# PV matmuls of two heads on the two column halves of TensorE, with one logarithm and one product for both

**Chip, cores, metric.** One core of a Trainium2 chip; runs of one round share a chip, and each is compared with the kernel before of its own rounds. The metric is the device time of one execution in microseconds (us), median of several.

**Names in the profile lines.** PE is TensorE's matmuls and PEld its weight loads; DVE is VectorE, ACT ScalarE, POOL GpSimd. L311 is line 311 of the kernel. PSUM is the memory to which the kernel's matmuls write; a bank is here one of the two [128 x 512] halves of o_ps. A timeline line gives start, duration (us), engine, line, operation, output<-input, shapes and count, and in brackets the idle time before it and what ended it. A wait line gives its total, how often it came and the longest. The end of a matmul record is modelled, so costs on TensorE are read from start to start.

## The reference

Sliding-window causal attention (window 64) over 8 batches x 8 heads x 576 positions x 64, then a multiplicative feed-forward network (FFN) on the 4608 x 512 result:

```python
scores = scale * q @ k.T;  mask: 0 <= i - j < 64
attn = exp(scores - max) / sum;   x = (attn @ v), heads side by side
out = ((x @ w1) * (x @ w2)) @ w3 @ w_out
```

## The kernel before

It folds `w3 @ w_out` into one matrix at the start, then runs attention and FFN interleaved. Attention goes in 48 **groups** (`d`), each two pairs of heads by 192 queries: `scores(d)` makes masked exponentials `pt`; `values(d)` makes PV (the exponentials times V) and softmax sums, and divides. The sum comes from 64 columns of ones that lie beside each head's V, in the order V0, ones, V1, ones. So a full 128-column weight gives head 0 with values on partitions 0 to 63 and sums on 64 to 127, and head 1 the other way round. Hence two logarithms and two products, each on 64 partitions. Division is `exp(-ln(sum))`.

```python
ps_t = ... bufs=1;  ps_s = ... bufs=1;  ps_v = ... bufs=1;  ps_f = ... bufs=3   # PSUM
# scores(d): two heads on the two halves of the ROWS of TensorE (64 x 128)
for a in range(2):
    nc.tensor.matmul(s_ps[:, a, jj, c0:c0 + n], kT[half, j, k0:k0 + P], qT[half, j, q0:q0 + n], ...)
... exponential on ACT, two masks on POOL ...
def values(d):
    ...
    o_ps = ps_v.tile([P, 2, 512], FP32, name="o_ps")
    for jj in range(2):
        first = True
        for a in range(2):
            c0 = 0
            for bi, (k0, q0, n, _) in enumerate(seg):
                o0 = a * 192 + q0 - q_base
                nc.tensor.matmul(o_ps[:, jj, o0:o0 + n],                       # L311
                                 v16[:, si * 2 + bi, j0 + jj, a * D:a * D + P],
                                 pt[:, a, jj, c0:c0 + n], start=first, ...)
                first = False
                c0 += n
    ...
    nc.scalar.activation(y[0:D], o_ps[D:P, :, 0:192], AF.Ln)                   # L320
    nc.scalar.activation(y[D:P], o_ps[0:D, :, 192:384], AF.Ln)                 # L321
    nc.scalar.activation(r, y, AF.Exp, scale=-1.0)                             # L323
    nc.vector.tensor_tensor(xs[0:D], o_ps[0:D, :, 0:192], r[0:D], ALU.mult)    # L326
    nc.vector.tensor_tensor(xs[D:P], o_ps[D:P, :, 192:384], r[D:P], ALU.mult)  # L327
# FFN: 8 matmuls of 512 columns each for w1/w2 (L395) and for the output (L408)
```

Groups 0 to 11 run in a startup with its own order of work; from group 12 on, a steady schedule has scores and PV half a cycle apart, with FFN matmuls between.

Of the kernel before, what the change touches and what calls it, by code (L numbers as in the profile page):

```python
# [11 lines left out]
ALU = mybir.AluOpType  # L12
AF = mybir.ActivationFunctionType
PSUM = bass.MemoryType.PSUM

P = 128
# [128 lines left out]
def kernel(  # L145
# [11 lines left out]
    nc = tc.nc  # L157
    B, H, S, D = q.shape
# [32 lines left out]
    xT = const.tile([P, NJ, RING], FP16)  # L191
# [104 lines left out]
    def values(d):  # L296
        b, r = divmod(d, 6)
        si, jp = divmod(r, 2)
        j0 = 2 * jp
        v16 = v16s[b % 2]  # L300
        pt = probs.pop(d)
        seg = SEGS[si]
        q_base = seg[0][1]
        o_ps = ps_v.tile([P, 2, 512], FP32, name="o_ps")
        for jj in range(2):
            first = True
            for a in range(2):
                c0 = 0
                for bi, (k0, q0, n, _) in enumerate(seg):
                    o0 = a * 192 + q0 - q_base  # L310
                    nc.tensor.matmul(o_ps[:, jj, o0:o0 + n],  # L311
                                     v16[:, si * 2 + bi, j0 + jj, a * D:a * D + P],
                                     pt[:, a, jj, c0:c0 + n],
                                     start=first, stop=(bi == 1), skip_group_check=True)
                    first = False
                    c0 += n
        if jp == 0:
            lns[b, si] = sb.tile([P, NJ, 192], FP32, name="ln_s", bufs=4)
        y = lns[b, si][:, j0:j0 + 2]
        nc.scalar.activation(y[0:D], o_ps[D:P, :, 0:192], AF.Ln)  # L320
        nc.scalar.activation(y[D:P], o_ps[0:D, :, 192:384], AF.Ln)  # L321
        r = sb.tile([P, 2, 192], FP32, name="r")
        nc.scalar.activation(r, y, AF.Exp, scale=-1.0)  # L323
        x0 = (b * S + q_base) % RING
        xs = xT[:, j0:j0 + 2, x0:x0 + 192]
        nc.vector.tensor_tensor(xs[0:D], o_ps[0:D, :, 0:192], r[0:D], ALU.mult)  # L326
        nc.vector.tensor_tensor(xs[D:P], o_ps[D:P, :, 192:384], r[D:P], ALU.mult)  # L327

    def keep_sums(n):
        b, si = divmod(n, 3)  # L330
# [25 lines left out]
    def tick(u):  # L356

        b, r = divmod(u, 12)
        d = u // 2
        if u % 2 == 0 and d < ND:  # L360
            scores(d)
        ev = late.get(r, [])
        for e in ev:
            if e[0] == "t":
                event(b, *e)
        if u % 2 == 1 and 12 <= d - 1 < ND:
            values(d - 1)
        for e in ev:
            if e[0] != "t":
                event(b, *e)  # L370
        n, m = divmod(u - LAG - 4, 4)
        if m == 3 and n >= 6:
            keep_sums(n)
# [158 lines left out]
    for d in range(5):  # L532
        if d == 0:
            w3Ts[2] = fold_t(2)
        values(d)
        if d < 4:
            scores(d + 2)
        fold_step(d + 2)
        if d == 0:
            load_v(1, 0, 2)  # L540
            load_qk(1, "k", nc.vector.memset)
            load_qk(1, "q")
        if d == 1:
            load_v(1, 3)
        if d == 2:
            copy_v(0, 4)
            for i in range(2):
                load_w12(i, 1)
        if d == 3:
            load_v(1, 4)  # L550
            cast_qk(1, "k", 0, dve_cp)
    cast_qk(1, "k", 1, act_cp)
    cast_qk(1, "q", 0, pool_cp)
    cast_qk(1, "q", 1, act_cp)
    values(5)
    fold_step(7)
    transposes(1, "k", 0, 1, into=spare(ps_s, "s_ps"))
# [113 lines left out]
```

## Time and profile before

| | before |
|---|---|
| median | 296.2 us (295.75 to 296.27) |
| span of the profiled run | 294.3 us |
| TensorE busy | 274.1 us, 93% |
| DVE / ACT busy | 185.4 / 168.4 us |

The costliest-groups list of the kernel before, the lines of `values` (line, engine, operation, output<-input, shapes, count | busy us, mean ns of one | idle before them and its releaser):

```profile
L326 DVE TENSOR_TENSOR xT<-o_ps,r 64x384 f16<-64x384 f32 x48 | 26.4, 550 | 53.8 <-ACT r L323 53.6
...
L320 ACT ACTIVATE ln_s<-o_ps 64x384 f32<-64x384 f32 x48 | 23.4, 487 | 53.4 <-PE o_ps L311 53.3
...
L311 PE MATMUL o_ps<-pt,v 128*128 128x128 f16 (+1 forms) x384 | 27.9, 215 | 5.9 <-DVE xT L327 4.0
...
L327 DVE TENSOR_TENSOR xT<-o_ps,r 64x384 f16<-64x384 f32 x48 | 26.9, 561 | 0.6
...
L321 ACT ACTIVATE ln_s<-o_ps 64x384 f32<-64x384 f32 x48 | 23.1, 482 | 0.5
```

The large idle times of DVE and ACT before these lines cost nothing: those engines are early. The one that counts is TensorE's 4.0 us before L311, waiting for L327.

### The profile page before, as it was taken

What the parts mean: (1) busy time and instruction counts of PE and PEld (TensorE: products, weight loads), DVE (VectorE), ACT (ScalarE), POOL (GpSimd) and SP (SyncE); (2) the same over time, 40 slices, a digit from 0 to 9 for tenths busy, and PEclk for the clock granted to TensorE, in tenths of its full rate; (3) what the DMA queues carried; (4) which work ended last, traced back from release to release, by engine and by line L of the source; (5) the groups of instructions that cost most, each with busy time, mean ns of one, the idle gap of its engine ahead of it and who ended that gap; (6) DMA issues with size and microseconds to landing.
All of it is one profiled execution on the core that took longest, in us unless ns stands there. A gap on an engine that the chain in (4) does not pass through costs nothing.

```text
span 294.3 us, 5925 instructions
## 1 busy us (share of the span) xinstructions
PE 274.1 (93%) x2254; PEld 152.9 (52%) x2254; DVE 185.4 (63%) x289; ACT 168.4 (57%) x281; POOL 180.8 (61%) x214
## 2 busy tenths in 40 slices
PE   7758889898799999999999999999999999999992
PEld 7544555444455555555555787555555445444440
DVE  0715688465787667687777866677867555554541
ACT  2513774676458647766686565487568866642300
POOL 8835995478749856696869463786595344402200
PEclk9999999999999999999999999999999999999998
DMA  6999999990277939094929470950094021012012
GB/s 231 219 181 201 265 278 212 373 131 36 74 266 264 72 110 321 39 85 143 322 20 100 136 295 2 155 73 1 20 171 40 0 74 72 0 38 109 0 57 95
DMA packets 51665, 38.85 MB, mean 132 GB/s; under 512 B 38784, under 2 KB 41856, under 8 KB 51632
## 3 DMA queue, kind: packets, MB, share of 16 engines
q0 software_dynamic: 41744, 9.96, 36.2%
q1 hardware_dynamic: 9888, 28.46, 26.6%
q8 instruction: 19, 0.31, 0.4%
q14 instruction: 14, 0.11, 0.1%
HBM read 38.80 MB, written 9.44 MB: 164 GB/s over the span
## 4 chain that ended last, share of the span: by engine, by line
PE 76%; DVE 6%; ACT 5%; DMA 4%; issue 3%; POOL 3%; POOLq 0%; DVEq 0%; ACTq 0%
PE f_ps L395 38%; PE f_ps L408 19%; PE o_ps L311 7%; PE tp L253 5%; DMA ab<-in_moe_w_dram 4%; PE s_ps L278 4%; DVE xT L327 2%; PE f_ps L454 2%; ACT ln_s L321 2%; ACT r L323 2%; POOL v L488 2%; DVE kT L257 1%; DVE xT L326 1%; ACT ln_s L320 1%; ACT pt L282 1%
## 5 line engine op out<-in xcount | busy, mean ns | idle before, releaser
L395 PE MATMUL f_ps<-xT,w_sb 128*128 128x512 f16 (+1 forms) x640 | 134.1, 358 | 0.0
L290 POOL TENSOR_SCALAR_AFFINE_SELECT pt<-pt 128x512 f16<-128x512 f16 (+1 forms) x64 | 52.1, 814 | 69.0 <-ACT pt L282 68.9
L395 PEld LDWEIGHTS <-w_sb 128*128 128x128 f16 x640 | 59.7, 98 | 50.7 <-issue 0.5
L408 PE MATMUL f_ps<-wc_sb,ab 128*128 128x512 f16 x288 | 67.1, 379 | 0.1
L401 DVE TENSOR_TENSOR ab<-f_ps,a_sb 128x512 f16<-128x512 f32 x72 | 49.8, 692 | 18.4 <-PE f_ps L395 15.8
L326 DVE TENSOR_TENSOR xT<-o_ps,r 64x384 f16<-64x384 f32 x48 | 26.4, 550 | 53.8 <-ACT r L323 53.6
L282 ACT ACTIVATE pt<-s_ps 128x1024 f16<-128x1024 f32 (+1 forms) x48 | 45.5, 949 | 18.0 <-PE s_ps L278 16.5
L400 ACT COPY a_sb<-f_ps 128x512 f32<-128x512 f32 x72 | 41.7, 579 | 24.8 <-PE f_ps L395 23.9
L292 POOL TENSOR_SCALAR_AFFINE_SELECT pt<-pt 128x512 f16<-128x512 f16 (+1 forms) x64 | 52.4, 819 | 4.4
L320 ACT ACTIVATE ln_s<-o_ps 64x384 f32<-64x384 f32 x48 | 23.4, 487 | 53.4 <-PE o_ps L311 53.3
L408 PEld LDWEIGHTS <-ab 128*128 128x128 f16 x288 | 26.9, 98 | 28.8 <-DVE ab L401 0.6
L233 POOL DMA_DIRECT2D v<-in_v_dram x40 | 33.9, 854 | 5.9 <-DMA ab<-in_moe_w_out_dram 4.1
L311 PE MATMUL o_ps<-pt,v 128*128 128x128 f16 (+1 forms) x384 | 27.9, 215 | 5.9 <-DVE xT L327 4.0
L311 PEld LDWEIGHTS <-v 128*128 128x128 f16 x384 | 23.5, 98 | 18.2 <-issue 3.5
L410 DVE COPY t2k<-f_ps 128x512 f32<-128x512 f32 x36 | 24.7, 690 | 11.6 <-PE f_ps L408 11.1
L327 DVE TENSOR_TENSOR xT<-o_ps,r 64x384 f16<-64x384 f32 x48 | 26.9, 561 | 0.6
L323 ACT ACTIVATE r<-ln_s 128x384 f32<-128x384 f32 x48 | 25.1, 523 | 1.5
L321 ACT ACTIVATE ln_s<-o_ps 64x384 f32<-64x384 f32 x48 | 23.1, 482 | 0.5
L278 PEld LDWEIGHTS <-kT 64*128 64x128 f16 x384 | 10.5, 94 | 16.5 <-issue 14.8
L278 PE MATMUL s_ps<-qT,kT 64*128 64x128 f16 (+1 forms) x384 | 18.2, 214 | 0.3 <-ACT pt L282 0.2
L257 DVE COPY kT<-tp 128x768 f16<-128x768 f16 x17 | 16.2, 952 | 0.1
L454 PE MATMUL f_ps<-ab,t2k 128*128 128x512 f16 x64 | 15.0, 379 | 0.4 <-DVE t2k L448 0.3
(59 smaller groups left out, 179.8 us busy)
## 6 DMA issues: line engine op xcount, KB each, us to landing
stage<-in_k_dram SPq DMA_DIRECT2D x16, 576.0 KB
stage<-in_q_dram SPq DMA_DIRECT2D x16, 576.0 KB
out_dram<-t2k SPq DMA_DIRECT2D x36, 256.0 KB
v<-in_v_dram POOLq DMA_DIRECT2D x32, 128.0 KB, 4.7
w_sb<-in_moe_w_dram POOLq DMA_DIRECT2D x4, 512.0 KB, 9.5
ab<-in_moe_w_out_dram POOLq DMA_DIRECT2D x1, 1024.0 KB, 10.6
ab<-in_moe_w_dram POOLq DMA_DIRECT2D x2, 512.0 KB, 12.6
xT<-in_moe_w_dram POOLq DMA_DIRECT2D x2, 512.0 KB, 16.2
```

What stands on the lines that cost most here:

```text
L233: nc.gpsimd.dma_start(out=vh[lo:P, c], in_=v[b, :, s0:s0 + P - lo, :].rearrange("h s d -> s h d"))
L278: nc.tensor.matmul(s_ps[:, a, jj, c0:c0 + n], kT[half, j, k0:k0 + P], qT[half, j, q0:q0 + n], start=True, stop=True, skip_group_check=True)
L282: nc.scalar.activation(pt[:, :, :, 0:w], s_ps[:, :, :, 0:w], AF.Exp, bias=-SHIFT, scale=scale)
L290: nc.gpsimd.affine_select(out=sl, in_=sl, pattern=pat, compare_op=ALU.is_ge, fill=0.0, base=off, channel_multiplier=-1)
L292: nc.gpsimd.affine_select(out=sl, in_=sl, pattern=[[-s, m] for s, m in pat], compare_op=ALU.is_ge, fill=0.0, base=63 - off, channel_multip ...
L311: nc.tensor.matmul(o_ps[:, jj, o0:o0 + n], v16[:, si * 2 + bi, j0 + jj, a * D:a * D + P], pt[:, a, jj, c0:c0 + n], start=first, stop=(bi = ...
L323: nc.scalar.activation(r, y, AF.Exp, scale=-1.0)
L327: nc.vector.tensor_tensor(xs[D:P], o_ps[D:P, :, 192:384], r[D:P], ALU.mult)
L395: nc.tensor.matmul(d[:, f * n + c0:f * n + c1], w[:, dc, (fc + f) * P:(fc + f + 1) * P], xT[:, dc, xc:xc + c1 - c0], start=first, stop=(dc ...
L400: act_cp(a_sb[:, 0:nf * n], a_ps[:, 0:nf * n])
L401: nc.vector.tensor_tensor(ab[:, fc:fc + nf, lo:hi], b_ps[:, 0:nf * n].rearrange("p (f n) -> p f n", f=nf), a_sb[:, 0:nf * n].rearrange("p ...
L408: nc.tensor.matmul(o_ps, ab[:, fc, t * P:t * P + P], wc_sb[:, fc, :], start=(fc == 0), stop=(fc == 7))
```

## The change

Each head's V and each head's ones become a 64-column weight of their own: head 0 on columns 0 to 63 of TensorE, head 1 on 64 to 127. Values of both heads go to one PSUM bank, sums to the other, on matching partitions. So one logarithm and one product serve both heads. The price is 16 half-wide matmuls and loads for 8 full ones.

```diff
         for jj in range(2):
-            first = True
-            for a in range(2):
-                c0 = 0
-                for bi, (k0, q0, n, _) in enumerate(seg):
-                    o0 = a * 192 + q0 - q_base
-                    nc.tensor.matmul(o_ps[:, jj, o0:o0 + n],
-                                     v16[:, si * 2 + bi, j0 + jj, a * D:a * D + P],
-                                     pt[:, a, jj, c0:c0 + n],
-                                     start=first, stop=(bi == 1), skip_group_check=True)
-                    first = False
-                    c0 += n
+            c0 = 0
+            for bi, (k0, q0, n, _) in enumerate(seg):
+                o0 = jj * 192 + q0 - q_base
+                for s in range(2):
+                    for a in range(2):
+                        nc.tensor.matmul(o_ps[a * D:a * D + D, s, o0:o0 + n],
+                                         v16[:, si * 2 + bi, j0 + jj, (2 * a + s) * D:(2 * a + s) * D + D],
+                                         pt[:, a, jj, c0:c0 + n],
+                                         start=(jj == 0 and bi == 0), stop=(bi == 1), skip_group_check=True)
+                c0 += n
...
-        nc.scalar.activation(y[0:D], o_ps[D:P, :, 0:192], AF.Ln)
-        nc.scalar.activation(y[D:P], o_ps[0:D, :, 192:384], AF.Ln)
+        nc.scalar.activation(y, o_ps[:, 1, 0:384].rearrange("p (j n) -> p j n", j=2), AF.Ln)
...
-        nc.vector.tensor_tensor(xs[0:D], o_ps[0:D, :, 0:192], r[0:D], ALU.mult)
-        nc.vector.tensor_tensor(xs[D:P], o_ps[D:P, :, 192:384], r[D:P], ALU.mult)
+        nc.vector.tensor_tensor(xT[:, j0:j0 + 2, x0:x0 + 192], o_ps[:, 0, 0:384].rearrange("p (j n) -> p j n", j=2), r,
+                                ALU.mult)
```

More of the change, by code (lines that the diff above doesn't have):

```diff
@@ L324, in values @@
         x0 = (b * S + q_base) % RING
-        xs = xT[:, j0:j0 + 2, x0:x0 + 192]
-        nc.vector.tensor_tensor(xs[0:D], o_ps[0:D, :, 0:192], r[0:D], ALU.mult)
-        nc.vector.tensor_tensor(xs[D:P], o_ps[D:P, :, 192:384], r[D:P], ALU.mult)
+        nc.vector.tensor_tensor(xT[:, j0:j0 + 2, x0:x0 + 192], o_ps[:, 0, 0:384].rearrange("p (j n) -> p j n", j=2), r,
+                                ALU.mult)
     def keep_sums(n):
```

## The prediction

> **What bounds the kernel now.** I read the page's busy shares and slices first, then the chain that ended last, then the busy times by stage, the PE waits, and at last the timeline of one steady stretch and of one startup stretch.
>
> ```profile
> PE 274.1 (93%) x2254; PEld 152.9 (52%) x2254; DVE 185.4 (63%) x289; ACT 168.4 (57%) x281; POOL 180.8 (61%) x214
> ...
> PE   7758889898799999999999999999999999999992
> ```
>
> TensorE is the one engine near full, and all its gaps lie in the first third. The table by stage says the same in microseconds (stretch, its length, then busy time of each engine with instruction counts, granted clock, DMA):
>
> ```profile
> 24.00:44.00 20.00, 17.32 (x172) 9.81 (x170) 13.98 (x26) 13.53 (x22) 16.91 (x20) 1.00 1.39 253
> ...
> 62.00:92.00 30.00, 26.37 (x233) 14.35 (x233) 21.21 (x34) 18.13 (x32) 22.30 (x26) 1.00 0.52 149
> 92.00:165.00 73.00, 73.00 (x590) 38.60 (x589) 54.03 (x84) 49.70 (x84) 56.48 (x65) 1.00 0.68 132
> 165.00:256.00 91.00, 91.00 (x755) 52.42 (x752) 60.54 (x95) 60.94 (x104) 52.64 (x64) 1.00 0.39 81
> ```
>
> From 92 to 256 us TensorE is busy 164 us of 164: in that steady part ACT and DVE have a quarter to a third of their time free, and relief for them is worth nothing by itself. From 24 to 92 us TensorE idles 7.5 us. What it waits for there (PE waits over the whole span):
>
> ```profile
> PE o_ps L311 <- DVE xT L327: 4.0, 9, 0.7
> ...
> PE tp L253 <- DVE kT L257: 1.2, 1, 1.2
> ```
>
> The PV group (L311) has one PSUM buffer, so the next PV waits until the second product (L327) has read the last one. All nine waits fall before 92 us: 1.7 us in 24 to 44, 2.3 us in 62 to 92. That is all the change can win directly. The startup loop, engine by engine:
>
> ```profile
> 29.72 0.50 PE L311 MATMUL o_ps<-pt,v 128*128 128x128 f16 x8 [0.26 <-DVE xT L327]
> ...
> 30.26 0.49 ACT L320 ACTIVATE ln_s<-o_ps 64x384 f32<-64x384 f32 x1 [0.93 <-PE o_ps L311]
> ...
> 30.76 0.48 ACT L321 ACTIVATE ln_s<-o_ps 64x384 f32<-64x384 f32 x1
> ...
> 31.27 0.52 ACT L323 ACTIVATE r<-ln_s 128x384 f32<-128x384 f32 x1
> ...
> 31.82 0.55 DVE L326 TENSOR_TENSOR xT<-o_ps,r 64x384 f16<-64x384 f32 x1 [0.92 <-ACT r L323]
> ...
> 32.39 0.56 DVE L327 TENSOR_TENSOR xT<-o_ps,r 64x384 f16<-64x384 f32 x1
> ...
> 33.10 0.61 PE L311 MATMUL o_ps<-pt,v 128*128 128x128 f16 x8 [0.27 <-DVE xT L327]
> ```
>
> The loop takes 3.38 us, and in it TensorE itself waits only 0.27 us: its own work in the loop is 3.11 us, just under the chain.
>
> Last, a steady stretch of TensorE, for what a change of tile shape costs:
>
> ```profile
> 91.78 1.89 PE L395 MATMUL f_ps<-xT,w_sb 128*128 128x512 f16 x8
> 93.60 0.40 PE L278 MATMUL s_ps<-qT,kT 64*128 64x128 f16 x8
> 93.93 0.51 PE L253 MATMUL tp<-ident,q 128*128 128x128 f16 x6
> 94.28 1.89 PE L395 MATMUL f_ps<-xT,w_sb 128*128 128x512 f16 x8
> 96.01 0.39 PE L311 MATMUL o_ps<-pt,v 128*128 128x128 f16 x4
> ...
> 93.60 0.23 PEld L278 LDWEIGHTS <-kT 64*128 64x128 f16 x8 [0.42 <-issue]
> ```
>
> From 94.28 to 96.01, eight FFN matmuls with no tile change take 1.73 us, 0.216 us each. From 91.78 to 93.60, the same eight before the 64-row score matmuls take 1.82: the change of tile costs 0.09 to 0.10 us. The eight scores run as four concurrent pairs of 128 columns; at a 128-column matmul's 0.056 us (six transposes, 93.93 to 94.28, are 0.35) that is 0.22, yet the next starts after 0.33: 0.11 us for the change back. The weight loads of L278 sit idle for 0.42 us ahead of the change: they aren't pulled ahead across it. So a visit to another tile shape costs 0.20 to 0.21 us of TensorE. PV today has the full shape, and pays none.
>
> **What the Trainium skill says.**
> 1. "TensorEngine Tiling (Array Packing)", Key Properties: a change of tiling mode, not of tile, drains TensorE. The trace agrees for the 64-row mode, 0.10 us each way. No 128x64 tile occurs before, so that it holds for column halves is taken from the page.
> 2. The same page, Restrictions: column tiling switches Fast Weight Load off. Not seen in the trace before. With it, eight full PV loads keep pace with 0.056 us matmuls.
> 3. "TensorE: Matmul & The Clock Gate", LDWEIGHTS: without it a load takes about columns/1.2 ns. My estimate from that page: 64 columns, 53 ns. Not seen in the trace before.
> 4. "ScalarE: Activation LUTs", What ACT_TABLE_LOAD costs: an activation with immediate scale takes 186 ns + 0.833 ns per element of the row, whatever the partitions; 384 elements would be 506 ns. The trace has 487 and 482 on 64 partitions, 523 on 128: the length of the row counts, not the partitions.
>
> **The change part by part.**
> - Logarithm: two of 64x384 (487, 482 ns) become one of 128x384, about 490 ns by the row's length. ACT loses 48 x 0.48 = 23 us; the PV chain gets 0.49 us shorter.
> - Product: two of 64x384 (550, 561 ns) become one of 128x384, about 560 ns. DVE loses 48 x 0.55 = 26 us; the chain gets 0.56 us shorter. PV to PV falls from 3.38 to about 2.33 us.
> - PV matmuls: 8 of 128x128 per group become 16 of 128x64, in pairs on the two halves, 768 for 384. The moving columns of a pair are those of one old matmul, so if pairs run side by side, as the score pairs do, the stream stays 8 x 0.056 = 0.45 us. Loads: 16 for 8. If the two halves load side by side, 53 ns lie under 56. I allow nothing for them in the centre beyond 0.03 to 0.05 us a group, since the margin is thin.
> - Tile changes: two more per group. Following the order of groups on TensorE, the changes of shape rise from 98 to 186: +88, since in startup scores follow PV directly and one change is shared there.
>
> Sum, steady part and tail (values from 95 us on, 34 groups, each between FFN groups): 34 x 0.205 = +7.0 us, all on the bounding engine, nothing beside it to hide behind. Loads there: 34 x 0.045 = about +1.5 us.
> Startup, 24 to 44 us: TensorE's own 3.11 becomes about 3.25 with one extra change; four steps of 3.38 to 3.50 save about 0.15 each, the last one (wait 0.70) about 0.6: -1.2 us. From 44 to 62 us: nothing (PV waits for the POOL masks). From 62 to 92 us: waits of 0.71, 0.71, 0.48, 0.38 give about 1.8 after the extra changes; the wait on kT copies, which stand behind the products on DVE, about 0.5; an earlier a_sb/ab near 68 us about 0.5: -2.8 us. Together -4.0 us.
> Net: +7.0 + 1.5 - 4.0 = +4.5 on 296.2, **300.7 us**; I say 301.
>
> **The rivals.**
> - *Weight loads bind.* If the two halves load one after the other, a pair takes 53 + 53 = 107 ns, not 56: +0.41 us a group, 36 groups out of startup +15 us, and the startup gain goes as well: about 318 us. For it: the fast load is off. Against it: the score pairs load and run at 26 ns a matmul, so issue is fast enough, and halves have their own paths by the pages. Chance 0.2; something in between (70 to 90 ns a pair, 304 to 310 us), another 0.2.
> - *No drain for column halves.* Then steady stays as it is, and only startup gains: 296.2 - 4 to 5 = 291 to 292 us, within 2%. For it: rows, not columns, are split in the only case the trace shows. The 48-row, one-column matmuls of the range check also wait, but they split both. Chance 0.12.
> - *ACT and DVE relief pays more.* It would if the steady part hid waits on f_ps buffers, and startup gained the whole 1.05 us at each of 11 steps. The PE waits of 92 to 256 us are empty, and startup's TensorE is itself at 3.1 of 3.4 us, so I don't believe it: at best 289 us, chance 0.05.
> - *POOL binds startup.* It is busy 16.9 of 20 us from 24 to 44; with shorter steps the masks (2.2 us per scores plus load issues) could take over as the wait. That takes back at most the 1.2 us gained there.
>
> **Range and chances.** Centre 301 with ideal or nearly ideal pairs (0.45), 291 to 292 without drains (0.12), 304 to 310 and 318 with loads exposed (0.4). The 2% limits are 290.3 and 302.1. Under 290.3: 0.05. Between: the no-drain case, and a little over three quarters of the ideal-pair case: 0.48. Over: 0.47. Range 292 to 316.
>
> **What would show it.** Right: PE stays at 9 in every slice from 92 us, the steady cycle (PV to PV, scores and two FFN groups, 4.67 us between 154.87 and 159.54) becomes about 4.9; PV's loads idle before each group as L278's do now; the FFN group ahead of PV takes 1.82 instead of 1.73 us; the one logarithm shows about 490 ns, the product 560; the L311 waits on DVE shrink from 4.0 to under 1 us; the first FFN work after startup starts some 3 us earlier. Wrong: PV to FFN taking 0.9 us or more (loads bind), the FFN group ahead of PV still at 1.73 (no drain), a new PE wait, or a steady cycle at or under 4.67 us.

## The result, and the profile after

**300.38 us** (299.1 to 301.0, four runs) against 296.18: ratio 1.0139, 95% interval 1.0105 to 1.0174, so slower by 1.4%. Every ratio here is the mean time of one kernel's runs over that of the other's of the same rounds, so not quite the ratio of the medians quoted. The profiled execution was the fastest of the four (299.1 us, span 297.3).

The costliest groups of the changed kernel (L312 is PV, L320 the logarithm, L324 the product):

```profile
L320 ACT ACTIVATE ln_s<-o_ps 128x384 f32<-128x384 f32 x48 | 23.6, 491 | 56.0 <-PE o_ps L312 56.0
L324 DVE TENSOR_TENSOR xT<-o_ps,r 128x384 f16<-128x384 f32 x48 | 26.8, 558 | 43.2 <-ACT r L322 43.1
...
L312 PEld LDWEIGHTS <-v 128*64 128x64 f16 x768 | 22.4, 110 | 21.5 <-issue 18.7
L312 PE MATMUL o_ps<-pt,v 128*64 128x128 f16 (+1 forms) x768 | 29.4, 218 | 2.3 <-POOL pt L292 1.6
```

One logarithm of 128x384 costs 491 ns, as one of 64x384 did (487); the product 558 for 550 and 561. ACT and DVE are relieved by 22.3 and 23.9 us (busy 146.1 and 161.5). The 18.7 us for which PV's loads sat idle with no wait that the profile shows ("issue") were 3.5 before. TensorE's waits for PV no longer name DVE's product:

```profile
PE o_ps L312 <- POOL pt L292: 1.6, 3, 0.8
...
PE o_ps L312 <- DVE v L239: 0.7, 1, 0.7
```

The stage table (stretch, length, busy of PE, PEld, DVE, ACT, POOL, granted clock, DMA) shows startup filled up, and the steady part as full as before:

```profile
24.00:44.00 20.00, 18.38 (x225) 10.55 (x224) 12.36 (x21) 11.07 (x17) 17.43 (x20) 1.00 1.38 252
...
62.00:92.00 30.00, 29.89 (x313) 16.12 (x311) 20.48 (x31) 17.29 (x28) 24.94 (x29) 1.00 0.72 169
92.00:165.00 73.00, 73.00 (x680) 36.77 (x675) 45.64 (x66) 41.01 (x66) 52.88 (x60) 1.00 0.65 131
165.00:256.00 91.00, 91.00 (x859) 49.53 (x858) 49.00 (x74) 49.74 (x82) 51.53 (x62) 1.00 0.38 77
```

And one steady cycle of the changed kernel (timeline; the last line is the weight loads' own row):

```profile
151.29 1.89 PE L393 MATMUL f_ps<-xT,w_sb 128*128 128x512 f16 x8
153.11 0.64 PE L312 MATMUL o_ps<-pt,v 128*64 128x128 f16 x16
153.68 1.90 PE L406 MATMUL f_ps<-wc_sb,ab 128*128 128x512 f16 x8
155.51 0.40 PE L278 MATMUL s_ps<-qT,kT 64*128 64x128 f16 x8
...
153.10 0.48 PEld L312 LDWEIGHTS <-v 128*64 128x64 f16 x16 [0.42 <-issue]
```

The FFN group ahead of PV takes 1.82 us (151.29 to 153.11) where it took 1.73, the PV group 0.57 (153.11 to 153.68) where it took 0.44 to 0.45, and PV's loads stand idle for 0.42 us, as those of the scores always did. PV to PV is 4.90 us for 4.67 in the same cycle of the kernel before.

How late (+) or early (-) each PV group starts against the kernel before, in us, aligned at group 1, from the start times of the matmuls in the traces (the other columns are experiments, below):

```
group   changed   hybrid14   two_logs   two_products   no_relief
  1       0.00       0.00       0.00        0.00          0.00
  5      -0.58      -0.61      +0.02       -0.44         +0.12
  8      -1.59      -1.75      -0.66       -0.82         +0.38
 11      -2.88      -3.03      -1.34       -1.80         +0.70
 13      -4.39      -4.55      -2.44       -2.17         +0.83
 20      -2.77      -4.40      -2.18       -2.02         +2.45
 30      -0.48      -4.40      -2.18       -2.02         +4.74
 46      +3.19      -4.40      -2.18       -2.02         +8.42
```

The change wins 4.4 us up to group 13 and then loses 7.58 us in 33 groups, 0.230 us in every one. (Group 1 itself started at 29.35 us for 29.72 in these two executions; without the alignment, group 13 is 4.75 us early.)

### The profile page after: what moved, and what is told of

Its sections match the earlier page's. It is cut to its first block, busy times and chain, and to the rows that moved or that the text cites. A ratio compares the mean times of both kernels' runs of the same rounds, so it can differ in the third digit from the quotient of the medians.

```text
span 297.3 us, 6567 instructions
## 1 busy us (share of the span) xinstructions
PE 283.8 (95%) x2638; PEld 154.1 (52%) x2638; DVE 161.5 (54%) x241; ACT 146.1 (49%) x233; POOL 180.9 (61%) x214
## 3 DMA queue, kind: packets, MB, share of 16 engines
q1 hardware_dynamic: 9888, 28.46, 26.1%
## 4 chain that ended last, share of the span: by engine, by line
PE 84%; POOL 7%; DMA 4%; DVE 1%; ACT 1%; issue 0%; POOLq 0%; DVEq 0%; ACTq 0%
PE f_ps L393 42%; PE f_ps L406 21%; PE o_ps L312 8%; PE tp L253 5%; PE s_ps L278 4%; DMA ab<-in_moe_w_dram 4%; POOL pt L290 2%; POOL pt L292 2%; PE f_ps L452 2%; POOL v L486 2%; PE s_ps L253 1%; POOL v L233 1%; ACT pt L282 1%; POOL w_sb L427 0%; POOL ab L431 0%
## 5 line engine op out<-in xcount | busy, mean ns | idle before, releaser
L393 PEld LDWEIGHTS <-w_sb 128*128 128x128 f16 x640 | 59.0, 98 | 52.5 <-issue 0.2
L320 ACT ACTIVATE ln_s<-o_ps 128x384 f32<-128x384 f32 x48 | 23.6, 491 | 56.0 <-PE o_ps L312 56.0
L324 DVE TENSOR_TENSOR xT<-o_ps,r 128x384 f16<-128x384 f32 x48 | 26.8, 558 | 43.2 <-ACT r L322 43.1
L312 PEld LDWEIGHTS <-v 128*64 128x64 f16 x768 | 22.4, 110 | 21.5 <-issue 18.7
L312 PE MATMUL o_ps<-pt,v 128*64 128x128 f16 (+1 forms) x768 | 29.4, 218 | 2.3 <-POOL pt L292 1.6
L214 POOL CAST q<-stage 128x1152 f16<-128x1152 f32 x13 | 14.6, 1147 | 0.0
L477 PE MATMUL tp<-ident 128*128 128x128 f16 x140 | 12.3, 267 | 2.2 <-POOL ident masks.py:199 1.5
```

The source lines that it names most:

```text
L312: nc.tensor.matmul(o_ps[a * D:a * D + D, s, o0:o0 + n], v16[:, si * 2 + bi, j0 + jj, (2 * a + s) * D:(2 * a + s) * D + D], pt[:, a, jj, c0 ...
L324: nc.vector.tensor_tensor(xT[:, j0:j0 + 2, x0:x0 + 192], o_ps[:, 0, 0:384].rearrange("p (j n) -> p j n", j=2), r, ALU.mult)
L393: nc.tensor.matmul(d[:, f * n + c0:f * n + c1], w[:, dc, (fc + f) * P:(fc + f + 1) * P], xT[:, dc, xc:xc + c1 - c0], start=first, stop=(dc ...
```

## The experiments

**The theory:** the steady loss is the change of TensorE's tile shape, twice a group, on an engine with no slack; the startup gain is the shorter PV chain. **Rivals:** the loss lies in doubled matmuls and loads; the gain lies elsewhere; the two depend on each other. All timed versions gave correct results. A row's "before" is from the same chip and rounds; compare rows by their ratios.

| run | median us | before, same rounds | ratio (95%) |
|---|---|---|---|
| hybrid14 | 291.17 | 296.83 | 0.981 (0.978 to 0.984) |
| hybrid14_rev | 304.39 | 296.83 | 1.025 (1.022 to 1.028) |
| no_relief | 305.25 | 296.83 | 1.029 (1.026 to 1.032) |
| halves_in_turn | 308.73 | 296.83 | 1.041 (1.038 to 1.044) |
| scores_beside_pv | 305.29 | 296.40 | 1.030 (1.028 to 1.031) |
| two_more_changes | 308.65 | 296.40 | 1.041 (1.040 to 1.043) |
| extra_same_shape | 297.49 | 296.40 | 1.003 (1.001 to 1.004) |
| after_again (changed kernel) | 300.21 | 296.40 | 1.012 (1.010 to 1.014) |
| hybrid14_two_logs | 293.71 | 296.55 | 0.990 (0.988 to 0.992) |
| hybrid14_two_products | 293.69 | 296.55 | 0.991 (0.989 to 0.994) |
| hybrid12 | 291.79 | 296.55 | 0.984 (0.982 to 0.987) |

### Gain and loss apart: hybrid14 and its mirror

The order of V and ones is the same in both kernels, so each group can choose its form.

```diff
+        if d < 14:          # hybrid14_rev: d >= 14
             ... column halves, one logarithm, one product ...
+        else:
+            ... full shape, two logarithms, two products, as before ...
```

> PV groups 0 to 13 (startup) on column halves with one logarithm and product, groups 14 to 47 (steady) in the old full shape with two of each. Theory (steady loss is the change of tile shape on a full TensorE, startup gain is the shorter PV chain, and the two are independent): the 4.75 us by which group 13 started earlier stays, nothing is lost after it: 296.2 - 4.75 = 291.4 us, and from group 13 on the distance to the kernel before stays constant. Rival (the early gain is an offset that later waits on ACT and DVE would eat up if they have their old load): 294 to 296 us, with PE waits in the steady part.

> The mirror: groups 0 to 13 old, 14 to 47 on halves. Theory: the startup gain is absent, the steady loss is whole: 296.2 + 34 x 0.223 = 303.8 us. Rival (the steady loss hangs on the startup having changed, such as another phase of FFN and PV or other DMA times): nearer 300.

Measured 291.17 and 304.39: the theory's numbers, within 0.3 and 0.6 us. Against the 296.83 of their own rounds that is -5.7 and +7.6, where -4.8 and +7.6 were expected. In the table of starts hybrid14 keeps its 4.40 us unchanged from group 20 to 46. Its stage table shows no stall taking the gain back:

```profile
62.00:92.00 30.00, 29.90 (x307) 16.28 (x305) 20.48 (x31) 17.24 (x29) 24.91 (x29) 1.00 0.70 169
92.00:165.00 73.00, 73.00 (x603) 40.09 (x602) 53.79 (x84) 49.26 (x83) 52.78 (x61) 1.00 0.67 140
165.00:256.00 91.00, 90.95 (x728) 50.56 (x726) 60.33 (x94) 60.27 (x103) 53.37 (x65) 1.00 0.35 68
```

ACT and DVE carry their old load there (49 and 54 us of 73), and TensorE still is full: relief is worth nothing in the steady part. Each effect appears without the other, and hybrid14 beats both kernels.

### Is the gain the logarithm and the product? no_relief

The changed kernel, with the merged operations split again:

```diff
-        nc.scalar.activation(y, <sums of both heads>, AF.Ln)
+        nc.scalar.activation(y[0:D], dn[0:D], AF.Ln)
+        nc.scalar.activation(y[D:P], dn[D:P], AF.Ln)
-        nc.vector.tensor_tensor(xT[...], <values of both heads>, r, ALU.mult)
+        nc.vector.tensor_tensor(xs[0:D], nu[0:D], r[0:D], ALU.mult)
+        nc.vector.tensor_tensor(xs[D:P], nu[D:P], r[D:P], ALU.mult)
```

> Column halves everywhere, but two logarithms of 64x384 and two products of 64x384 as before. Theory (the startup gain comes from one logarithm and one product less in the chain): steady +7.6, startup gain gone and the extra changes partly on the chain (0 to +1): 303.8 to 305 us. Rival (the gain comes from sums in a bank of their own, or from PV itself): stays at 300.4.

Measured 305.25. Group 13 starts 0.83 us late instead of 4.39 early, and the steady loss is the same 0.23 a group. TensorE's nine waits for the second product are back as well (4.0 us in the kernel before):

```profile
PE o_ps L312 <- DVE xT L329: 3.8, 9, 0.7
```

So the gain is these two operations, and no gain from the separate bank for sums shows. The steady loss does not depend on the relief either.

### Do the halves run at the same time? halves_in_turn

```diff
-                for s in range(2):
-                    for a in range(2):        # a innermost: neighbours on different halves
+        for a in range(2):                    # a outermost: eight of head 0, then eight of head 1
+            for jj ...: for bi ...: for s ...:
```

> The changed kernel, but all eight matmuls of head 0 (first half of the columns) ahead of all eight of head 1, so that no neighbours lie on different halves. Same count, same loads, same changes of shape. Theory (neighbours on the two halves run at the same time, as score pairs do): the stream of a group doubles, 0.45 to 0.90 us for two segments in three, 0.34 to 0.67 for the third: +0.41 us a group, 34 groups +14 us, startup 0 to +5: 314 to 319 us. Rival (a group's time is set by issuing 32 instructions or by loading 16 weights, not by streaming): 300.4 unchanged.

Measured 308.73: right in direction, too small for the theory's size. In the timeline a PV group lasts 0.82 us (157.40 to 158.22), not the expected 0.90 plus 0.10 for the change back:

```profile
157.40 0.89 PE L312 MATMUL o_ps<-pt,v 128*64 128x128 f16 x16
158.22 0.39 PE L406 MATMUL f_ps<-wc_sb,ab 128*128 128x512 f16 x1
```

The single starts show what happened. In the changed kernel a group's sixteen matmuls start at 0, 3, 80, 83, 135, 139, 191, 195, ... ns: pairs 3 to 4 ns apart, a new pair every 56 ns. In halves_in_turn they start at 0, 80, 136, 191, 247, **253**, 303, 333, 359, 389, 415, 445, 501, 556, 612, 668 ns. Matmuls of 128 columns on one half are 56 ns apart, so the one at 253 runs on the other half, beside the first head's last four. In groups with unequal pieces the widths prove it. In program order each head has 128, 128, 64, 64, 128, 128, 64, 64 columns; the trace has 128, 128, 64, 64, 128, 128, 128, 128, 64, 64, 64, 64, 128, 128, 64, 64. The second head's first matmuls started before the first head was through. So the halves do run side by side: about half of each head's eight overlapped, even though they weren't written alternately. It was TensorE that put the second head's matmuls forward, not the compiler: built again from this run's kernel, the compiled program for TensorE has the first head's eight ahead of the second's in all 48 groups.

### What does a change of shape cost? two_more_changes and its control

```diff
+                if jj == 1 and bi == 0:      # middle of the PV group, unread columns of the sums' bank
+                    nc.tensor.matmul(o_ps[:, 1, 400:402], ident16, ident16[:, 0:2], start=False, ...)
```

The control, extra_same_shape, is the kernel before with the same matmul in the middle of its full-shape groups (into bank 0).

> The changed kernel with one full-shape matmul of two columns, into unread columns of the sums' bank, in the middle of each PV group: two more changes of shape a group. Theory: 34 x 2 x 0.11 = 7.5 us and some 0.03 to 0.05 us a group for the matmul itself, startup 0 to 3: 309 to 312 us. Rival (a change of shape is nearly free, what costs is something else in the group): about 302, like the control.

> Control: the kernel before with the same two-column matmul in the middle of each of its full-shape PV groups. No change of shape. All theories: 48 x 0.03 to 0.05 us: 297 to 298.5 us.

Measured 308.65 against 300.21 of the changed kernel in the same rounds, and 297.49 against 296.40. The group in two_more_changes, then one of the control:

```profile
153.75 0.36 PE L315 MATMUL o_ps<-pt,v 128*64 128x128 f16 x8
154.05 0.18 PE L311 MATMUL o_ps<-ident 128*128 128x2 f16 x1
154.15 0.36 PE L315 MATMUL o_ps<-pt,v 128*64 128x128 f16 x8
154.45 1.90 PE L396 MATMUL f_ps<-xT,w_sb 128*128 128x512 f16 x8
```

```profile
156.67 0.39 PE L314 MATMUL o_ps<-pt,v 128*128 128x128 f16 x4
156.89 0.17 PE L308 MATMUL o_ps<-ident 128*128 128x2 f16 x1
156.92 0.38 PE L314 MATMUL o_ps<-pt,v 128*128 128x128 f16 x4
```

The two-column matmul is followed by PV after 0.03 us where the shape stays, after 0.10 where it changes. From group 13 to 46 the control falls 0.86 us behind the kernel before, 0.026 a group. The version with two more changes falls 7.62 us behind the changed kernel (first profile), 0.231 a group. So one change costs (0.231 - 0.026)/2 = 0.10 us, by an addition that alters nothing else; half of the 0.024 us by which the second half's first pair is late again (below) is in it. The total landed just under the expected range (309 to 312): 34 x 0.231 is 7.9 us where 8.5 to 9.2 were expected, and startup cost 1.6 us up to group 13, within the 0 to 3 allowed. (The profiled execution, its slowest, took 309.87.)

### One change fewer: scores_beside_pv

```diff
-        if u % 2 == 0 and d < ND:
-            scores(d)
         ...
         if u % 2 == 1 and 12 <= d - 1 < ND:
             values(d - 1)
+        if u % 2 == 1 and d < ND:
+            scores(d)
```

> The changed kernel, with the scores of the steady part issued right behind a PV group instead of half a cycle earlier, so that TensorE goes full, columns, rows, full: three changes of shape a cycle for four. Nothing else is removed. Theory (each change costs about 0.11 us wherever it lies): 34 x 0.11 = 3.7 us less: 296.7 us, cycle 4.78 for 4.89. Rival (the loss belongs to PV's doubled matmuls and loads): 300.4 unchanged. It could also go wrong by PV waiting for the masks of later scores; then a wait of PV on POOL shows.

Measured 305.29, so worse, by the way out that the expectation named: scores come later, their masks come later, and PV waits for them.

```profile
PE o_ps L312 <- POOL pt L292: 8.8, 24, 0.8
```

Locally the theory holds: the undisturbed cycles took 6.52 for 6.62, or 4.74 for 4.84 us, 0.10 less for the one change saved. As a version it fails, and since 24 waits lie over it, its total decides nothing.

### The repeat

> The changed kernel again, unedited, for the comparison on this chip and because its four runs spread over 1.9 us (299.1 to 301.0) where the kernel before spread over 0.5. Expected 300.4; the startup until the weights have landed, or the granted clock, should be what differs between its executions, not the steady cycle of 4.89 us.

Median 300.21 (299.07 to 300.53). Each of its cycles from group 14 on is, within 0.01 us, that of the first profile, so the steady part does not vary. What moves the total by over 1 us between executions of this kernel is not shown: a typical execution was not profiled, only ones of 299.1 and 299.2 us. (The spread is not peculiar to this kernel: in hybrid14's rounds the kernel before went from 295.61 to 297.79.)

The traces of other runs give a lead, and it is the granted clock that the expectation named. In most of the profiles TensorE ran at half clock for some 3.4 us (6.8 in no_relief) once in the startup: from 13.6 to 17.0 us in the changed kernel's, at no time in the startup of the kernel before once it had full clock, at 4.8 us. In hybrid12, extra_same_shape and scores_beside_pv the spell began at about 21 us. There the sixteen 512-column matmuls that fold the weights took 5.31 us instead of 3.63 (the slow ones started 427 ns apart instead of 216), and the first PV group started at 26.4 to 26.7 us instead of 25.2 to 25.4. Those executions lie 1.3, 1.2 and 0.3 us above the medians of their kernels. It is not the only cause: the profile of two_more_changes, 1.2 us above its median, had its spell at 13.3 us and its first PV at 26.1. Whether such a spell lengthened the slower executions of the changed kernel, no profile shows.

### Which half of the relief? hybrid14_two_logs, hybrid14_two_products, hybrid12

hybrid14, in groups 0 to 13, with the two logarithms put back, or the two products; and hybrid14 with the switch at 12.

> The split version (groups 0 to 13 on halves) with the two logarithms of 64x384 back in these groups, one product. Theory (the PV chain, now about 2.3 us, is shorter than TensorE's own 3.17 us a step from 26 to 44 us, so half of the relief is enough): the chain becomes 2.8 us, still under 3.17; only the two steps of 2.63 and 2.73 us between 60 and 73 us lose 0.1 to 0.2 each: 291.3 to 291.7 us against 291.2. Rival (each part of the relief is worth its own duration at each of some 10 waits): 0.48 x 10 back at most, 294 to 296.

> The same with one logarithm and the two products of 64x384 back in groups 0 to 13. Theory as for the logarithms: 291.3 to 291.7, and up to 0.5 more because the kT copies near 78 us stand behind the products on DVE: up to 292.2. Rival: 294 to 296.

> Groups 0 to 11 on halves, 12 to 47 in the old shape. Groups 12 and 13 lie behind the startup. Theory: group 12 had no wait before and saves its two changes, 0.2 us; group 13 had a wait of 0.38 us for the products of 12, which comes back but saves its two changes: 291.0 to 291.4 us, the same as the version with 14 within noise.

Measured 293.71, 293.69 and 291.79. The last is 0.4 us above its range, and its ratio agrees with hybrid14's within the intervals, so 12 or 14 makes no clear difference. The others lie 0.3 us under the rival's range and some 2 us above the theory's: the theory failed. Each half costs back some 2.5 us of hybrid14's 5.7. My reckoning looked at the PV chain alone. The PE waits of two_logs, then of two_products:

```profile
PE o_ps L313 <- POOL pt L292: 2.0, 3, 1.2
```

```profile
PE o_ps L313 <- DVE xT L328: 1.2, 2, 1.0
PE tp L253 <- DVE kT L257: 1.0, 1, 1.0
```

The second logarithm also delays the exponentials that stand behind it on ACT. The POOL masks of group 5 then end at 42.9 instead of 42.5 us, and TensorE waits 1.19 us for them, not 0.79. The second product delays the kT copies near 78 us (wait 0.98), and group 5 waits 0.97 us for the product itself, which there stands behind a cast on DVE. The two losses don't lie at the same groups (table of starts).

## Why the prediction was right, point by point

- **Total.** 301.0 predicted, 300.38 measured, inside the range, in the class within 2% that I had given 0.48. Slower by over 2% had 0.47: too much, since it rested on exposed loads. That the median came so close is partly luck: both terms of the sum were too high, by 0.75 and 0.9 us, and some 1.2 us that the profiled pair does not show made up for most of that (see Net).
- **The steady part.** Predicted 0.25 us a group (changes 0.205, loads 0.045) or 8.5 us over 34; measured 0.230 and 7.6. Read from single starts: FFN to PV 0.310 instead of 0.216 us is 0.094 for the change in; the first pair takes 0.080 instead of 0.056, so 0.024, which I put down to its exposed load; the last pair to FFN takes 0.155 instead of 0.056, so 0.10 for the change back; and the FFN group behind PV takes 1.833 instead of 1.822, 0.011 more. Together 0.229. The cost read from the row-split scores carried over to column halves. The loads term was about twice too large.
- **Rival: loads bind.** Refuted. The first two loads of one half start 28 ns apart, and those of the two halves 3 ns apart. As a pace, my estimate of 53 ns was about double, and pairs start every 56 ns after the first, as full matmuls did, so the loads bind nowhere but at the first pair.
- **Rival: no drain for column halves.** Refuted by the 0.094 and 0.10 us, and by two_more_changes.
- **Startup.** Predicted -4.0 us by the end; measured -4.75 at group 13 (91.44 to 86.69 us), 0.37 of it there by group 1. By stage: to group 5 -0.95 (predicted -1.2), to group 7 another -0.27 (predicted 0), then -3.53 (predicted -2.8). The loop step fell from 3.38 or more to 3.08 and 3.17 us (29.35 to 32.43 and 32.43 to 35.60 in the changed kernel), where TensorE itself binds it; I had 3.25. Here the prediction misread the wait: its 0.27 us counts from the modelled end of the last FFN matmul. From starts, FFN to PV took 2.16 us (30.94 to 33.10) where eight such matmuls take 1.73, so TensorE waited 0.43 us and had 2.95 us of work of its own, not 3.11. The three steps after group 1 therefore saved 0.30, 0.30 and 0.22 us instead of 0.15 each; the last, expected to save 0.6, lost 0.24 to a wait for the masks, so that -0.95 for -1.2 is a sum of misses. The last term was too small mainly at the kT copies: the wait of 1.2 us for them is gone whole, where 0.5 was allowed, and from group 11 to 12 the lead grows by 1.10 us. two_products shows the link: with the second product ahead of these copies on DVE, a wait of 0.98 us for them is back.
- **Rival: POOL binds startup.** True at one group: the 0.8 us wait for masks at group 5 let the lead shrink from 1.19 us at group 4 to 0.95.
- **Net.** -4.75 and +7.6 make about +3 in the profiled pair of executions (spans 294.3 and 297.3), +4.2 in medians. The remaining 1.2 us (the profiled execution was the fastest of its four, 299.10 for a median of 300.38) is the open point of the repeat.

## What to carry to other kernels

Read a merge of small operations by stage: it helps where the engine that bounds the end waits for their chain, and nowhere else. If it is paid for on the bounding engine, in every pass, it can lose where everything else got lighter; the better version is then the new form where there are waits and the old form where there are none (here 291.2 us against 296.8 in the same rounds; 300.2 for the changed kernel in others). Here two half-wide matmuls on different halves were as cheap as one full one (a pair, like a full matmul, started every 56 ns), but each visit to another tile shape cost TensorE 0.2 us: count the visits, not the matmuls. And read a wait on TensorE from starts: the profile's idle time of 0.27 us was 0.43.

## What the Trainium skill lacked or had wrong

- "TensorEngine Tiling (Array Packing)", Key Properties: it says that a change of tiling mode drains TensorE, but gives no cost. Here: 0.094 us into the 128x64 shape, 0.10 us back, and 0.024 us for the first 64-column load; some 0.10 us each way for 64x128 rows.
- "TensorE: Matmul & The Clock Gate", LDWEIGHTS: columns/1.2 ns would be 53 ns for 64 columns. Here the first two loads of one half started 28 ns apart, on both halves at once, while the record of one lasts 106 to 113 ns: neither its pace nor its length is 53.
- "TensorE: Matmul & The Clock Gate", Part 3, The mechanism: it has matmuls start strictly in program order. In halves_in_turn, the first matmul of the second column half started at 253 ns, ahead of three of the first half that come before it in the compiled program (303, 359 and 415 ns).
